# Reordering first loads and sums, merging a normalization, and doing sums on two tiles at a time, in a transformer block bound by the matrix engine

## The chip, the cores and the metric

One core of a Trainium2 chip runs the whole kernel. The metric is the device time of one execution in microseconds (us). PE is TensorE (matmuls; PEld its weight loads), DVE is VectorE, ACT is ScalarE, POOL is GpSimd, SP is the engine that issues most DMAs. Every execution in this document but one was in the fast state (granted TensorE clock 0.999 or 1.0); the exception is named where it comes.

## The reference, cut to what matters

```python
def reference(A_x, A_wqkv, A_wo, B_x, B_w_gate, B_w_up, B_w_down):
    # x is 2048 x 1024 bf16; 32 heads; a window of 8 keys with dilation 2; feed-forward width 3584
    h  = x + attention(layernorm(x))  @ wo
    h2 = h + ((layernorm(h) @ w_gate) * (layernorm(h) @ w_up)) @ w_down
    return h2
```

The kernel works in four chunks of 512 rows. It does part of the feed-forward products with Strassen-like sums: 7 products of half-size blocks in place of 8, at the price of sums of weight blocks and of activation blocks. Those sums are the subject here.

## The kernel before: the parts concerned

The start loads four row tiles on SP's queue and the first weight block in two halves on ACT's queue, then normalizes, transposes (on PE) and copies one row tile after the other.

```python
    for t in range(4):
        load_x0(t)
    load_w0(0, 4)                                   # ACT's queue
    nc.scalar.preload_act_table_set("natural_log_exp_and_others")
    load_w0(4, 4)                                   # ACT's queue
    # ... 13 warm-up matmuls ...
    def first_rstd(t):
        nc.vector.bn_aggr(out=mv0[:, t, :], in_=sts[t][:])
        rstd_of(mv0, rs0, t, t + 1)                 # Ln and Exp on ACT

    def first_norm(t):
        lns[t] = lnp.tile([128, D], BF, tag="ln", name=f"ln0_{t}")
        for i in range(2):
            cols = bass.ts(i, 512)
            nc.vector.tensor_scalar(lns[t][:, cols], x0[t][:, cols], mv0[:, t, 0:1], rs0[:, t:t + 1],
                                    ALU.subtract, ALU.mult)

    def first_transpose(t):
        for hf in range(2):
            # ... 4 transposes of 128 x 128 on PE into pt ...
            nc.scalar.copy(lnTs[0][:, bass.ts(hf, 4), bass.ts(t, 128)], pt[:])
```

The head of the pair stage. `weight_sums` scales a weight block on ACT and makes four sums of its quarters on DVE; `activation_sums` makes four sums of the quarters of the transposed, normalized rows, which come from DMA transposes. `result` reads a PSUM tile, adds, and stores the output.

```python
    for q in range(2):
        dprod(ex[q], q, EF["21"], fcells(dn["12"]), False)
        # ...
    retire(1)
    activation_sums(l2, l3, dn["px"])
    weight_sums(0, nc.vector)
    for q in range(2):
        dprod(ey[q], q, EF["12"], fcells(dn["22"]), False)
        nc.vector.tensor_tensor(p5t[:, q, :], p5t[:, q, :], hs1[q][:, 512:1024], ALU.add)
        result(1, hs1[q], q, 1, ey[q], dn["inv"], p5t[:, q, :])
    for q in range(2):
        dprod(ex[q], q, EF["22"], fcells([dn["kx"], dn["vx"]]), False)
        result(1, hs1[2 + q], 2 + q, 0, ex[q], dn["inv"], None)
```

The last stage. `HA` holds 14 tiles of 128 x 512 in each of four quadrants; `HF` are the same bytes as f16.

```python
    for k in range(NP):                             # NP = 14
        to_f16(HF["22"][k], HA["22"][k], sh)        # DVE
        to_f16(HF["21"][k], HA["21"][k], sh)
    # ... conversion of "11" on ACT; S1 = HF21 + HF22 on DVE, 14 sums ...
    for q in range(4):
        dprod(ps_x[q], q, HA["12"], fcells(down["b21"]), False)
        result(2, hs2[q], q, 0, ps_x[q], scale_d.inv, None)
    for k in range(NP):
        nc.vector.tensor_tensor(HF["21"][k], HF["11"][k], HF["21"][k], ALU.subtract)
    for k in range(NP):
        nc.vector.tensor_tensor(HF["11"][k], S1[k], HF["11"][k], ALU.subtract)
    sub(t2h, down["b22"], t1h)                      # prodx, two halves
    # ... four products with S1 ...
    for q in range(4):
        dprod(ps_y[q], q, HF["11"], fcells(t2h), False)        # "dy"
```

## Time and profile before

| | before |
|---|---|
| time, median of 5 runs | 779.04 us (778.85 to 779.19) |
| span of the profiled run | 777.6 us |
| PE busy | 770.7 us, 99% |
| DVE / ACT busy | 614.9 us, 79% / 473.8 us, 61% |

The page cuts the span into 40 slices; each digit is a tenth of busy time, and the second line is the granted clock.

```profile
PE   8999999999999999999999999999999999999998
...
PEclk9999999999999999999999999999999999999999
```

PE is never visibly idle but in the first and the last slice. What can be won without taking matmuls away is therefore small, and it must be looked for in single waits. A matmul of 512 columns is drawn 0.379 us long though the next one starts 0.216 us after it, so a busy PE hides short waits. Where this document says that PE **lost** time at a place, it is worked out from start times: start of the matmul, less start of the one before, less 0.216 us (0.056 us for 128 columns). Beyond 18 us, the trace before has losses of over 0.03 us in five places only: 0.14 at 60.6 us, 1.04 and 0.39 ahead of the two `pv` products at 520 us, 0.24 and 0.43 in the first `dy` product at 725 us.

The chain that ended last (start, us, what):

```profile
694.99 18.14 PE dx L787 x84
...
718.60 2.01 DVE hq L1066 x6
...
727.22 10.73 PE dy L787 x49
```

The chain runs on PE up to 713.1, leaves it for DVE, and comes back to PE at 727.22. That detour is the place where the kernel waits for sums.

### The profile page before, as it was taken

Reading aid. Unit: us, or ns where it says so; the run is one execution under the profiler, and the core shown is the slowest. Engines: PE = TensorE matmul, PEld = TensorE weight load, DVE = VectorE, ACT = ScalarE, POOL = GpSimd, SP = SyncE. Lnnn points to the kernel's source line nnn. Section 1 sums busy time; section 2 is a strip of 40 time slices with the busy share of each in tenths; the row PEclk is TensorE's granted clock in tenths of the full one; section 3 lists DMA queues with packets and bytes.
Section 4 is the critical chain, followed back from the end, with each engine's and each line's share of the span. In section 5 each row is a group of like instructions: output and inputs, shape, how many; then the busy total and the mean of one; then the engine's idle time right before and its main releaser. Section 6 shows DMA issues by size and latency. Waiting matters only on the chain.

```text
span 777.6 us, 10495 instructions
## 1 busy us (share of the span) xinstructions
PE 770.7 (99%) x3707; PEld 355.1 (46%) x3707; DVE 614.9 (79%) x805; ACT 473.8 (61%) x1029; POOL 142.3 (18%) x152
## 2 busy tenths in 40 slices
PE   8999999999999999999999999999999999999998
PEld 6544444444444444444444444444444444444444
DVE  6619999999899999999988989985553444579862
ACT  4627445323476661976769899746677677788240
POOL 0000000010000200002000001008778687600000
PEclk9999999999999999999999999999999999999999
DMA  8999693895965868867645384744332423730001
GB/s 275 258 217 222 158 291 88 255 305 130 338 205 167 269 228 239 267 225 259 207 150 192 120 298 121 162 96 111 106 97 67 109 62 101 248 131 28 1 27 55
DMA packets 181605, 133.86 MB, mean 172 GB/s; under 512 B 79024, under 2 KB 174384, under 8 KB 179504
## 3 DMA queue, kind: packets, MB, share of 16 engines
q1 hardware_dynamic: 176912, 110.12, 50.1%
q0 software_dynamic: 3584, 22.02, 8.1%
q10 hardware_dynamic: 1056, 1.05, 0.4%
q8 instruction: 29, 0.48, 0.3%
q14 instruction: 24, 0.20, 0.1%
HBM read 104.86 MB, written 22.02 MB: 163 GB/s over the span
## 4 chain that ended last, share of the span: by engine, by line
PE 88%; DVE 9%; DMA 1%; ACT 1%; issue 0%; SPq 0%; ACTq 0%; DVEq 0%
PE ps L392 20%; PE pg L392 12%; PE pu L392 12%; PE dx L787 6%; PE pz L680 6%; PE acc L626 6%; PE py L680 6%; PE px L680 6%; PE wo L513 4%; PE pv L680 3%; PE dy L787 3%; DVE h L834 1%; DMA w_qkv<-in_A_wqkv_dram 1%; PE ps L353 1%; PE ex L787 1%; DVE prodx L780 1%
## 5 line engine op out<-in xcount | busy, mean ns | idle before, releaser
L392 PE MATMUL ps<-lnT,w_qkv 128*128 128x512 bf16 x736 | 159.8, 379 | 0.0
L392 PEld LDWEIGHTS <-w_qkv 128*128 128x128 bf16 x736 | 71.8, 98 | 86.0 <-issue 0.3
L392 PE MATMUL pg<-lnT,w_wg 128*128 128x512 bf16 x448 | 105.8, 379 | 0.0
L392 PE MATMUL pu<-lnT,w_wu 128*128 128x512 bf16 x448 | 105.8, 379 | 0.0
L304 ACT CAST sg<-ps 128x512 bf16<-128x512 f32 x96 | 54.8, 590 | 52.7 <-PE ps L392 50.0
L475 DVE TENSOR_TENSOR pv<-vD,at 128x4096 bf16<-128x4096 bf16 x32 | 72.5, 2287 | 0.3
L432 DVE TENSOR_TENSOR prod<-qD,kD 128x4096 bf16<-128x4096 bf16 x32 | 72.3, 2284 | 0.1
L680 PEld LDWEIGHTS <-sw 128*128 128x128 f16 x448 | 43.8, 98 | 54.3 <-issue 1.7
L392 PEld LDWEIGHTS <-w_wg 128*128 128x128 bf16 x448 | 43.8, 98 | 52.9
L392 PEld LDWEIGHTS <-w_wu 128*128 128x128 bf16 x448 | 43.8, 98 | 52.9
L596 ACT CAST us<-pu 128x512 bf16<-128x512 f32 x56 | 33.2, 593 | 40.5 <-PE pu L392 40.4
L680 PE MATMUL px<-lnT,ws 128*128 128x512 bf16 x224 | 55.2, 379 | 0.0
L680 PEld LDWEIGHTS <-ws 128*128 128x128 f16 x336 | 32.9, 98 | 39.6
L626 PE MATMUL acc<-w_wd,gs 128*128 128x512 bf16 x224 | 48.5, 379 | 0.0
L487 POOL DMA_DIRECT2D od<-oD x4 | 2.2, 544 | 252.8 <-DVE oD L485 162.5
L661 POOL TENSOR_TENSOR sw<-ws 128x512 f16<-128x512 f16 x26 | 30.0, 1153 | 85.4 <-PE py L680 78.2
L185 ACT ACTIVATE rs<-mv,eps 128x1 f32<-128x1 f32 (+1 forms) x25 | 7.4, 297 | 52.6 <-DVE mv L182 49.2
L591 ACT CAST gs<-pg 128x512 bf16<-128x512 f32 x56 | 32.9, 587 | 10.7 <-PE pg L392 8.7
L434 DVE TENSOR_TENSOR prod<-prod 128x4096 bf16<-128x4096 bf16 x16 | 36.6, 2288 | 0.3
L541 ACT ACTIVATE junkd<-w_wd 128x512 bf16<-128x512 bf16 x56 | 34.3, 618 | 0.0
L626 PEld LDWEIGHTS <-gs 128*128 128x128 bf16 x224 | 21.9, 98 | 26.4
L697 ACT COPY py<-px 128x512 f32<-128x512 f32 x28 | 16.0, 570 | 26.2 <-PE px L680 26.2
(312 smaller groups left out, 1400.5 us busy)
## 6 DMA issues: line engine op xcount, KB each, us to landing
w_wg<-in_B_w_gate_dram SPq DMA_DIRECT2D x14, 1024.0 KB, 6.7
w_wu<-in_B_w_up_dram SPq DMA_DIRECT2D x14, 1024.0 KB, 5.4
w_wd<-in_B_w_down_dram SPq DMA_DIRECT2D x8, 896.0 KB, 8.8
w_pair<-in_B_w_gate_dram SPq DMA_DIRECT2D x14, 512.0 KB, 4.1
w_pair<-in_B_w_up_dram SPq DMA_DIRECT2D x14, 512.0 KB, 5.4
w_wo<-in_A_wo_dram SPq DMA_DIRECT2D x6, 1024.0 KB, 8.1
w_qkv<-in_A_wqkv_dram SPq DMA_DIRECT2D x5, 1024.0 KB, 9.1
kd<-sg SPq DMA_DIRECT2D x32, 144.0 KB, 3.0
```

What stands on the lines that cost most here:

```text
L304: nc.scalar.copy(sg[:, HB:HB + TC], ps[:])
L392: nc.tensor.matmul(ps[:], lhsT=wt[:, ko, bass.ts(j, 128)], rhs=rhs[:, ko, :], start=(ko == 0), stop=(ko == KO - 1))
L432: nc.vector.tensor_tensor(prod[:, j], qD[:], kD[:, :, o:o + SUB], ALU.mult)
L434: nc.vector.tensor_tensor(prod[:, :, 0:16], prod[:, :, 0:16], prod[:, :, 16:32], ALU.add)
L475: nc.vector.tensor_tensor(pv[:, j], vD[:, :, o:o + SUB], at[:, w, None, :].to_broadcast((128, DH, SUB)), ALU.mult)
L513: nc.tensor.matmul(ps[:], lhsT=oTs[c][:, kk, t, :], rhs=wts["wo", c, hf][:, kk, :], start=(kk == 0), stop=(kk == KO - 1))
L541: nc.scalar.activation(junk, src, ACTF.Abs, accum_out=self.l1[:, k:k + 1])
L591: nc.scalar.copy(gs[:], pg[:])
L596: nc.scalar.copy(us[:], pu[:])
L626: nc.tensor.matmul(acc[t][:], lhsT=hT[f][:, bass.ts(t, 128)], rhs=wts["wd", c, hf, b][:, j, :], start=(f == 0), stop=(f == NF - 1))
L680: nc.tensor.matmul(ps[:], lhsT=lhs[:, ko, :], rhs=rhs[:, ko, :], start=(fresh and ko == 0), stop=(ko == 3), skip_group_check=not fresh)
L787: nc.tensor.matmul(ps[:, bass.ds(lo, n)], lhsT=lhs[k][:, bass.ts(q, 128)], rhs=rhs[k][:, bass.ds(lo, n)], start=(fresh and k == 0), stop=( ...
```

## The change

Its intent: issue both weight halves before ACT is given the table load; normalize row tiles 1 to 3 in one instruction instead of two; let the first weight sums, whose inputs are ready sooner, go ahead of the activation sums on DVE; and handle those of the last stage's tiles that lie in pairs (3 pairs in each quadrant, 8 single tiles) two at a time, to save instructions.

```diff
     load_w0(0, 4)
+    load_w0(4, 4)
     nc.scalar.preload_act_table_set("natural_log_exp_and_others")
-    load_w0(4, 4)
@@ first_norm
-        for i in range(2):
-            cols = bass.ts(i, 512)
+        for cols in (bass.ts(0, 512), bass.ts(1, 512)) if t == 0 else (slice(0, D),):
@@ head of the pair stage
+    weight_sums(0, nc.vector)
     activation_sums(l2, l3, dn["px"])
-    weight_sums(0, nc.vector)
@@ last stage
+    GA = {k: HA[k][0:8] + [ht[:, r::4, :] for ht in rooms] for r, k in enumerate(("11", "21", "12", "22"))}
+    GF = {k: [f16(a) for a in GA[k]] for k in GA}
+    NG = len(GA["11"])
...  (conversions and the sums into S1 likewise; G1 is S1 with its last six tiles as three pairs)
-    for k in range(NP):
-        nc.vector.tensor_tensor(HF["21"][k], HF["11"][k], HF["21"][k], ALU.subtract)
-    for k in range(NP):
-        nc.vector.tensor_tensor(HF["11"][k], S1[k], HF["11"][k], ALU.subtract)
+    for k in range(NG):
+        nc.vector.tensor_tensor(GF["21"][k], GF["11"][k], GF["21"][k], ALU.subtract)
+    for k in range(NG):
+        nc.vector.tensor_tensor(GF["11"][k], G1[k], GF["11"][k], ALU.subtract)
```

## The prediction

> **What bounds the kernel now.** I read the page first, then the list of PE's waits, then the chain that ended last, then the timeline of the three places where PE waits. The engine line and the list of waits say almost all of it:
>
> ```profile
> PE 770.7 (99%) x3707; PEld 355.1 (46%) x3707; DVE 614.9 (79%) x805; ACT 473.8 (61%) x1029; POOL 142.3 (18%) x152
> ...
> PE warm_ps L298 <- DVE warm L284: 1.2, 1, 1.2
> PE pv L680 <- DVE h L792: 1.1, 2, 0.9
> PE ps L353 <- ACT lnT L348: 0.3, 1, 0.3
> PE pt L347 <- DVE ln L340: 0.3, 1, 0.3
> PE ps L353 <- DMA w_qkv<-in_A_wqkv_dram: 0.3, 1, 0.3
> PE dy L787 <- DVE prodx L780: 0.3, 1, 0.3
> ```
>
> The columns of the waits are total us, how many, longest. TensorE is the bound everywhere: granted clock 1.00, matmuls 0.216 us apart (8 take 1.73 us in the chain), and only some 3.5 us of waiting shown in 777.6. A page's busy PE hides short waits, because a 512-wide matmul is drawn 0.379 us long while the next starts 0.216 us after it; so I work with start times below. The diff has no matmul added or removed, and the comparison of the instruction streams shows PE's order unchanged. The change can therefore win only what PE waits in three places: the start, the head of the pair stage (pv), and the last stage (dy).
>
> The pair stage's head, from the timeline of that stretch (start, length, what, idle before and its releaser):
>
> ```profile
> 507.38 3.69 ACT L654 ACTIVATE ws<-w_pair,sbgu 128x4096 f16<-128x4096 bf16 x1
> ...
> 511.90 1.23 DVE L672 TENSOR_TENSOR prodx<-lnT,lnT 128x2048 f16<-128x2048 bf16 x1 [2.19 <-DMA out_dram<-h]
> ...
> 516.57 0.69 DVE L661 TENSOR_TENSOR sw<-ws 128x1024 f16<-128x1024 f16 x1
> ...
> 519.89 0.75 DVE L792 SCALAR_TENSOR_TENSOR h<-ey,inv_h1d,ep 128x512 bf16<-128x512 f32 x1
> ...
> 520.69 1.02 PE L680 MATMUL pv<-prodx,sw 128*128 128x512 f16 x4 [0.88 <-DVE h L792]
> ...
> 522.81 1.02 PE L680 MATMUL pv<-prodx,sw 128*128 128x512 f16 x4 [0.23 <-DVE h L792]
> ```
>
> The scaled weights ws are ready at 511.07 (507.38 + 3.69), but DVE stands idle from 509.7 to 511.90, because next in its order are the activation sums, whose inputs (the transposed rows of chunk 3, last issued at about 509.8) have not landed. The releaser is printed as an output store; transposes of the same queue take 3.1 to 3.6 us to landing, so I take it for them. Then DVE runs without a gap: four sums, four weight sums, an add, and the result h at 519.89, which empties the PSUM bank that pv needs. PE could have begun pv at 519.65 (517.92 + 8 x 0.216) and begins at 520.69.
>
> The start and the end, same columns; the last two lines are from the chain (start, us, what):
>
> ```profile
> 11.44 0.73 DVE L340 TENSOR_SCALAR ln<-x,mv,rs 128x512 bf16<-128x512 bf16 x2 [0.37 <-ACT rs L186]
> 11.91 0.72 PE L347 MATMUL pt<-ident,ln 128*128 128x128 bf16 x8
> 12.35 1.07 ACT L348 COPY lnT<-pt 128x512 bf16<-128x512 bf16 x2 [0.94 <-PE pt L347]
> 13.31 0.31 ACT L185 ACTIVATE rs<-mv,eps 128x1 f32<-128x1 f32 x1
> ...
> 722.62 0.67 DVE kx L1066 x2
> 723.30 3.88 DVE prodx L780 x2
> ```
>
> At the start each row tile goes round a loop: normalize, transpose, copy, then the next tile's Ln and Exp on ScalarE, then normalize. It turns in 2.44 us (copies at 9.91, 12.35, 14.79). At the end DVE, busy from 713.16, finishes prodx at 727.17, and dy's eighth matmul starts at 727.22.
>
> **What the Trainium skill says.** (1) "VectorE: DVE Perf Modes", in the section on the TRN2 errata, gives SBUF operations a fixed cost per instruction, about 58 + elements/accel cycles at 0.96 GHz. For a two-source 16-bit add (accel 2) that is 0.327 us for 512 and 0.594 for 1024. The trace agrees: adds of 512 follow each other every 0.335 us (two in 0.67, above), adds of 1024 every 0.605 (weight sums). (2) "Perfetto Trace Analysis", section Optimizing Scalar/DVE Operations, says that larger operations help a saturated engine, but that where an engine only causes bubbles on others, breaking instructions up may finish work sooner. The second half applies to the start, and the change does the opposite there. (3) "ScalarE: Activation LUTs", section What ACT_TABLE_LOAD costs, has about 1283 ns for the load and 1380 ns of drain. The trace has 1.28 us for the load (at 1.24), but the second weight DMA was issued at 1.27, beside it, not after it. (4) "DMA: Bandwidth & Descriptors", section Issuing engines are not separate DMA queues, says that all issues end on the same 16 engines; the trace shows 370 to 410 GB/s while x and the first weights load.
>
> **The change part by part.**
>
> *Weight block ahead of the table load.* The first half's issue takes 0.75 to 1.21, so the second can go at about 1.21 instead of 1.27: 0.06 us. It landed at 8.98, 7.7 us after its issue, with the 2 MB of x and weights that share the engines; the bandwidth sets that, not the issue. The table load moves to about 1.7 and ends at 3.0, while the first Ln runs at 5.60. **Worth 0.0.**
>
> *Normalizing in one instruction for tiles 1 to 3.* The two halves end 0.73 us after their start, the first after 0.405; one instruction of 1024 takes 0.539 (median of the same operation at line 190). The second half is 0.19 earlier, the first 0.135 later, and PE's transposes and the copies begin with the first. Tile 1: normalize starts at 8.93, so the transposes could go at 9.40 and go at 9.48, when PE has finished the matmuls that the weight DMA held; now 8.93 + 0.54 + 0.065 = 9.535, +0.055. Tile 2: 11.44 + 0.055 + 0.605 = 12.10 for 11.91, +0.19. Tile 3: 13.88 + 0.19 + 0.605 = 14.68 for 14.35, +0.33. The shorter second half wins nothing, since the second copy waits for ScalarE (0.48 us behind the first) and not for its transposes. All later matmuls move along. **Costs 0.33.**
>
> *Weight sums ahead of the activation sums.* DVE starts when ws is ready, 511.12, not at 511.90. Four weight sums take 2.54 (516.57 to 519.11), so the activation sums run from 513.66, when their inputs have long landed, and take 4.67 (511.90 to 516.57). The add starts at 518.33 for 519.11: 0.78 earlier, and so do h and the following results. pv starts at 519.91 (its slot is 519.65), the second pv at 522.03 for 522.81 (its slot would be 521.64). PE's loss here falls from 1.43 (1.04 + 0.39) to 0.65. **Worth 0.78**, and PE runs without a wait from there to the last stage, so it is kept.
>
> *Sums on two tiles at a time.* 6 of the 14 tiles of each quadrant become 3 pairs. Conversions on DVE: two of 512 cost 0.54 (hq: 12 in 3.23), one of 1024 about 0.40, so 6 pairs save 0.8; the first sums save 0.2; ScalarE's conversions 0.2 (1.24 to 1.17 a pair). All this lies before 713.16, where DVE waits 1.08 us for PE's last product whatever it saved, so it is worth nothing. Behind it lie two loops on the path, lines 1064 and 1066: 3 pairs each, 0.67 becoming 0.605: 6 x 0.065 = 0.39. prodx ends at 724.84 and 726.78. dy's first matmul then starts in its slot, 725.04 (was 725.28), and its eighth at 726.83 for 727.22; the slot would be 726.55. **Worth 0.39.** The fourth loop (line 1087, 750.75 to 755.4) is wanted only at 761.96 and is hidden.
>
> Sum: +0.33 - 0.78 - 0.39 = -0.84. From 779.04: **778.2 us**.
>
> **The rivals.** (a) *The start wins instead.* If the weight half came distinctly sooner, PE would do its 8 held matmuls sooner. But tile 1 then waits for the one-piece normalize at 9.535, so it can bring nothing; only if a 1024 normalize gave its result sooner than 0.54 us would the start be even: total 777.9. (b) *The activation sums become the wait at pv.* They end at 518.33 instead of 516.57, but the slot of pv is 519.65, so 1.3 us remain; a slip of the weight conversion on ScalarE would eat the gain directly: 779.0 if all is lost. (c) *Strided pairs lose the fast mode.* The pair tiles have two rows of 512 spaced 2048 apart. Line 661 already reads strided pieces of 128 at 0.605 for 1024, which speaks against it. If it happened, 6 adds would take about 1.1 instead of 0.605 and the end would lose about 2.6: 781.2. (d) *Everything moves within noise*: 779.0. Nothing here makes 2% (15.6 us); all PE waits together are about 3.5.
>
> **Range and chances.** The three terms have errors of about 0.2 each, and the runs before spread over 0.34. With the start even, 777.9 or a little less; with half of the pair's gain lost, 778.6. I take 777.6 to 778.8. Within 2%: 0.985.
>
> **What would show each step.** Right: DVE's first weight sum at about 511.4 (511.1 plus the start's 0.33), pv's wait under 0.3, dy's wait smaller, the copies of the first row tiles at 9.97, 12.54 and 15.12, the first 512-wide matmul at 17.54 instead of 17.21. Wrong: copies still 2.44 apart (then the merged normalize costs nothing); the weight half landing well before 8.9; a weight sum still starting after 511.9; adds of 2 x 512 at over 0.7; or a new PE wait in the last stage.

## The result, and the profile after

| | before | after |
|---|---|---|
| median of 5 runs | 779.04 us | 778.30 us |
| lowest to highest | 778.85 to 779.19 | 778.02 to 778.39 |
| span of the profiled run | 777.6 us | 776.5 us |

The changed kernel is 0.74 us faster by the medians. A ratio here is the mean time of one kernel's fast runs over that of the other's in the same rounds, so not quite the ratio of the medians: 0.999, with a 95% interval of 0.9975 to 1.0005. By that interval alone it is "the same"; the two sets of five runs do not overlap, though, and the traces say where the 0.74 lies.

PE's waits in the changed kernel (total us, how many, longest), to be held against the six lines in the prediction:

```profile
PE warm_ps L298 <- DVE warm L284: 1.2, 1, 1.2
PE ps L352 <- ACT lnT L347: 0.5, 1, 0.5
PE pv L679 <- DVE h L791: 0.2, 1, 0.2
```

The wait at `pv` went from 1.1 us in two pieces to 0.2 in one, and the one at `dy` is no longer listed (0.25 us is still lost there, hidden under the drawn length of the matmul before). The timeline of the pair stage's head:

```profile
507.48 3.69 ACT L653 ACTIVATE ws<-w_pair,sbgu 128x4096 f16<-128x4096 bf16 x1
...
511.20 0.69 DVE L660 TENSOR_TENSOR sw<-ws 128x1024 f16<-128x1024 f16 x1 [1.39 <-ACT ws L653]
...
513.74 1.22 DVE L671 TENSOR_TENSOR prodx<-lnT,lnT 128x2048 f16<-128x2048 bf16 x1
...
519.20 0.75 DVE L791 SCALAR_TENSOR_TENSOR h<-ey,inv_h1d,ep 128x512 bf16<-128x512 f32 x1
...
520.00 1.02 PE L679 MATMUL pv<-prodx,sw 128*128 128x512 f16 x4
```

DVE now starts as soon as ACT has the scaled weights (507.48 + 3.69 = 511.17), and the first activation sum at 513.74 no longer waits for its transposes. The result `h` comes at 519.20 instead of 519.89, `pv` at 520.00 instead of 520.69. PE's slot for it was 519.78 (first `px` at 518.05 plus 8 x 0.216), so 0.23 us is still lost, and 0.39 at the second `pv`.

The start, same columns as before:

```profile
11.44 0.55 DVE L339 TENSOR_SCALAR ln<-x,mv,rs 128x1024 bf16<-128x1024 bf16 x1 [0.62 <-ACT rs L186]
...
12.05 0.62 PE L346 MATMUL pt<-ident,ln 128*128 128x128 bf16 x8
...
12.48 1.07 ACT L347 COPY lnT<-pt 128x512 bf16<-128x512 bf16 x2 [1.07 <-PE pt L346]
...
14.62 0.62 PE L346 MATMUL pt<-ident,ln 128*128 128x128 bf16 x8
```

The normalization starts at 11.44 in both traces, but the transposes come 0.61 us later instead of 0.47, and the loop turns in 2.57 us (12.05 to 14.62) instead of 2.44 (11.91 to 14.35).

The chain at the end:

```profile
715.88 0.60 DVE hq_o L1069
716.48 0.60 DVE lx L1069
717.09 0.60 DVE kx L1069
...
722.18 3.88 DVE prodx L779 x2
...
726.10 10.73 PE dy L786 x49
```

Each pair takes 0.60 us of the chain where two tiles took 0.67, so a 2 x 512 pair with its strided rows runs at the rate of a plain 1024.

Setting matmul n of one trace against matmul n of the other (both have 3707, in the same order) gives the whole difference by place: +0.26 us up to the first 512-wide matmul (17.21 to 17.47), -0.14 at 60.6, -0.81 at `pv`, -0.42 at `dy`, in sum -1.11, the difference of the two spans. The -0.14 is at a place that the change does not edit (what varies there is told at the end of the point-by-point part); the trace before is one of the slower runs of its kernel (779.41 us). The experiments tell what of this is the change.

### The profile page after: what moved, and what is told of

It reads as the page before. It is cut to its first block, busy times and chain, and to the rows that moved or that the text cites. A ratio compares the mean times of both kernels' runs of the same rounds, so it can differ in the third digit from the quotient of the medians.

```text
span 776.5 us, 10462 instructions
## 1 busy us (share of the span) xinstructions
PE 771.1 (99%) x3707; PEld 355.5 (46%) x3707; DVE 612.6 (79%) x784; ACT 472.6 (61%) x1023; POOL 142.1 (18%) x152
## 4 chain that ended last, share of the span: by engine, by line
PE 90%; DVE 9%; ACT 1%; issue 0%; DVEq 0%
PE ps L391 20%; PE pu L391 12%; PE pg L391 12%; PE dx L786 6%; PE pz L679 6%; PE acc L625 6%; PE py L679 6%; PE px L679 6%; PE wo L512 4%; PE pv L679 3%; PE dy L786 3%; DVE h L833 1%; PE ps L352 1%; PE ex L786 1%; DVE prodx L779 1%; DVE w_dn L779 1%
```

## The experiments

Four kernels each carry one part of the change alone. Each was timed in five rounds beside the kernel before on the same chip. All differences are far below 2%, and only the intervals of after_halves, best and best_mid lie wholly below 1. For the single parts the gain or cost is therefore read from the places in the traces; the medians only agree with it.

**w_only.** The weight block's second half ahead of the table load, nothing else.

```diff
     load_w0(0, 4)
+    load_w0(4, 4)
     nc.scalar.preload_act_table_set("natural_log_exp_and_others")
-    load_w0(4, 4)
```

> Before, with the weight block's second half issued ahead of the table load and nothing else. Theory (each part acts in its own place, the wait for the weight half is set by the shared DMA bandwidth): the second half lands at 8.85 to 8.98 us instead of 8.98, PE's wait before its second group of first matmuls shrinks by at most 0.1, tile 1's transposes start at 9.40 to 9.48, and the time is 0.0 to 0.1 us shorter. Rival (the table load held the issue up, so the half comes much sooner): it lands before 8.5 and the time falls by 0.3 or more.

Measured: 779.19 us against 779.14 (ratio 1.0003, interval 0.999 to 1.0016): no change. PE, which waits for the half at this place, went on at 8.75 us, and in the other traces in which it stands there it went on at 8.42, 8.46, 8.47, 8.92, 8.97 and 9.03 with the old order and at 8.47, 8.53 and 8.92 with the new. The list of waits names the weight DMA in four of these traces only, so some of the times are upper bounds for the landing. The landings themselves, which the traces also hold, were at 8.71 here, 8.37 to 8.98 in the seven traces with the old order, and 8.10 to 8.88 in the other five with the new. The two orders share one spread of half a microsecond, and no gain of the new order is to be seen in it; a gain of 0.1, the most that was expected, is below what these runs resolve. This trace also lost 0.57 us at 60.7, where the trace before lost 0.14: scatter in a place that was not edited.

**norm_only.** The normalization of tiles 1 to 3 in one instruction, nothing else.

```diff
-        for i in range(2):
-            cols = bass.ts(i, 512)
+        for cols in (bass.ts(0, 512), bass.ts(1, 512)) if t == 0 else (slice(0, D),):
```

> Before, with the normalization of tiles 1 to 3 in one instruction and nothing else. Theory: it costs 0.25 to 0.35 us, because the transposes wait for the whole row: they start about 0.6 us after the normalization's start instead of 0.47, for tiles 2 and 3 (12.05 and 14.62 instead of 11.91 and 14.35), and the first 512-wide matmul starts at about 17.47 to 17.54 instead of 17.21. Rival (a shorter total lets the next tile start sooner): the loop stays at 2.44 us or less and the time is the same or up to 0.2 shorter.

Measured: 779.49 us against 779.14, 0.35 longer by the medians (ratio 1.0005, interval 0.9992 to 1.0019), though the two sets of runs overlap. Its timeline:

```profile
11.47 0.55 DVE L339 TENSOR_SCALAR ln<-x,mv,rs 128x1024 bf16<-128x1024 bf16 x1 [0.62 <-ACT rs L186]
...
12.07 0.45 PEld L346 LDWEIGHTS <-ln 128*128 128x128 bf16 x8 [0.17 <-DVE ln L339]
...
14.64 0.45 PEld L346 LDWEIGHTS <-ln 128*128 128x128 bf16 x8 [0.17 <-DVE ln L339]
```

The last column names the new wait: PE stands 0.17 us for the whole row, twice. From the first matmul of tile 1 to the first 512-wide matmul there are 6.92 or 6.93 us in the three traces with the merged normalization (this one, the changed kernel's two) and 6.66 in the nine that have it in halves and are otherwise alike there. **At the start this part of the change costs 0.26 to 0.27 us, against its intent**, and that is the steadiest figure.

**sums_only** and **sums_only_2.** The weight sums ahead of the activation sums, nothing else.

```diff
+    weight_sums(0, nc.vector)
     activation_sums(l2, l3, dn["px"])
-    weight_sums(0, nc.vector)
```

> Before, with the pair's first weight sums ahead of its activation sums and nothing else. Theory: 0.78 to 0.83 us shorter; PE's lost time ahead of the two pv products falls from 1.04 + 0.39 to about 0.25 + 0.39, and no other wait appears. Rival (the activation sums, now last, become the wait, or the gain is given back later in the pair stage): under 0.4 us shorter, with a PE wait on an activation sum or a weight sum of the next block.

The first run's profiled execution took 1015.66 us at a granted clock of 0.753. That execution counts in no ratio and says nothing of the waits. The median of 778.47 us counts it; the four fast executions alone have a median of 778.35 against 779.14. The same kernel was run once more.

> The first run's profile fell at a granted clock of 0.753, so it says nothing of the waits: the same kernel (before, with only the weight sums ahead of the activation sums) once more for a trace in the fast state. Theory: 0.6 to 0.85 us shorter; PE's lost times at pv 0.2 to 0.3 and 0.39, against 0.7 to 1.04 and 0.39 in the traces with the old order; no wait that the other traces don't have; the dy waits of 0.24 and 0.43 unchanged. Rival: a new wait in the pair stage takes over half of the gain back.

Measured: 778.35 against 778.96 us, 0.61 shorter; the four fast executions of the first run were 0.79 shorter. The new trace's waits:

```profile
PE dy L787 <- DVE prodx L780: 0.3, 1, 0.3
PE pv L680 <- DVE h L792: 0.2, 1, 0.2
```

PE lost 0.23 and 0.39 us at `pv`, exactly as in the changed kernel, and the `dy` waits are untouched (0.24 and 0.43). No other wait took over, so the rival falls. What varies is the old order: in its seven traces the first `pv` lost 1.04, 1.01, 0.92, 0.90, 0.90, 0.81 and 0.71 us, because there DVE waits for the DMA transposes and they land at slightly different times (DVE idle 1.86 to 2.19 us ahead of the first activation sum, which starts 0.28 us after the last transpose has landed in every one of the seven). The mean is 0.90, so the reordering is worth 0.90 - 0.23 = 0.67 us on average and up to 0.81 against the slowest trace. It also takes the scatter away: with the new order the loss is 0.23 or 0.24 in all four traces.

**pairs_only.** All sums and conversions of the last stage on two tiles at a time, nothing else (the diff above, last part).

> Before, with all sums and conversions of the last stage on two tiles at a time and nothing else. Theory: 0.39 to 0.43 us shorter, all of it at the head of the dy products (PE's lost time there 0.67 before, about 0.25 now). Rival (less work on VectorE, 2.3 us of busy time in all, is what counts): 0.8 us or more shorter, with the product before it starting or ending sooner too.

Measured: 778.64 us against 779.14, 0.50 shorter by the medians, though the two sets of runs overlap. PE lost nothing at the first matmul of `dy` and 0.25 at the eighth, against 0.24 and 0.43. To see which sums carry this, the pairing was split in two:

**pairs_on_path**: only the two subtraction loops behind the stage's last result are paired; conversions, sums into S1 and the last loop stay single.

```diff
-    for k in range(NP):
-        nc.vector.tensor_tensor(HF["21"][k], HF["11"][k], HF["21"][k], ALU.subtract)
-    for k in range(NP):
-        nc.vector.tensor_tensor(HF["11"][k], S1[k], HF["11"][k], ALU.subtract)
+    for k in range(NG):
+        nc.vector.tensor_tensor(GF["21"][k], GF["11"][k], GF["21"][k], ALU.subtract)
+    for k in range(NG):
+        nc.vector.tensor_tensor(GF["11"][k], G1[k], GF["11"][k], ALU.subtract)
```

> Before, with only the two subtraction loops behind the last product of the stage (those that make the left side of dy) on two tiles at a time. Theory: these two loops are all that counts of the pairing: 0.39 to 0.43 us shorter, as with all of it. Rival (the conversions and the first sums carry the gain): no change.

**pairs_off_path**: the other way round, these two loops single and all the rest paired.

> Before, with only the conversions, the first sums and the last subtraction loop on two tiles at a time, the two loops on the path left single. Theory: VectorE has about 1.7 us less to do, its idle time ahead of the stage's last result grows by about 1 us, and the time stays within 0.1 of before; PE still loses 0.67 at dy. Rival: 0.3 or more shorter.

Measured in the same rounds: pairs_on_path 778.22, pairs_off_path 778.88, before 778.88 us. The first keeps the gain at `dy` (0.25 lost), the second has none of it (0.24 and 0.43 lost) and no change of the time. The 0.66 of the first is more than the 0.42 that its trace shows at `dy`; the rest is the scatter of some 0.2 between sets of runs. DVE's timeline in pairs_off_path shows where the saved work went:

```profile
708.48 2.07 DVE L792 SCALAR_TENSOR_TENSOR h<-dx,ibd,h 128x512 bf16<-128x512 f32 x3
712.61 0.75 DVE L792 SCALAR_TENSOR_TENSOR h<-dx,ibd,h 128x512 bf16<-128x512 f32 x1 [2.06 <-PE dx L787]
```

and before:

```profile
710.02 2.06 DVE L792 SCALAR_TENSOR_TENSOR h<-dx,ibd,h 128x512 bf16<-128x512 f32 x3
713.16 0.75 DVE L792 SCALAR_TENSOR_TENSOR h<-dx,ibd,h 128x512 bf16<-128x512 f32 x1 [1.08 <-PE dx L787]
```

This trace is 0.55 us ahead of the other at this place. Beyond that, DVE is done about a microsecond sooner and waits that much longer (2.06 instead of 1.08 us) for PE's last product. Saved work ahead of a wait turns into wait.

**after_halves.** The changed kernel with the normalization in halves again, that is, without the part that costs.

```diff
-        for cols in (bass.ts(0, 512), bass.ts(1, 512)) if t == 0 else (slice(0, D),):
+        for i in range(2):
+            cols = bass.ts(i, 512)
```

> The changed kernel with the normalization of tiles 1 to 3 in halves again. Theory: 0.25 to 0.35 us shorter than the changed kernel, so 1.0 to 1.1 shorter than before; the first 512-wide matmul starts at 17.1 to 17.25. Rival (merged and split cost the same, the 0.26 shift seen in the changed kernel's trace came from its warm-up matmuls): no difference to the changed kernel.

Measured: 777.73 us against 778.88 before: 1.15 shorter (ratio 0.9986, interval 0.9974 to 0.9999), 0.4 more than the changed kernel gains. Its first 512-wide matmul was at 16.69, sooner than expected, but so it was in before_again; the whole start moves with the landing of the first row tile (DVE's first statistics began anywhere between 3.52 and 4.03 us in 13 traces). The duration within the start, 6.66 us, is what tells.

**before_again.** The kernel before, unchanged, as a control.

> The kernel before, unchanged, as a control of what one trace differs from another. Theory: PE's lost times at pv (1.04 and 0.39) and at dy (0.24 and 0.43) come back within 0.03, while the 0.14 lost at 60.6 and the landing of the weight half (8.98) move by 0.1 or so. Rival (the places differ from run to run as much as the change moved them): pv or dy differ by 0.2 or more.

Measured: 778.70 us against 778.88 in the same rounds, which is how far two medians of one kernel differ here. PE lost 1.01 and 0.38 at `pv`, 0.25 and 0.43 at `dy`, and nothing at 60.6. The control agrees within 0.03, but that was luck for the first `pv`, as the six other traces with the old order show.

**after_again.** The changed kernel once more.

> The changed kernel once more, on the same chip and in the same rounds as the two versions to compare with it. Theory: 0.7 to 0.8 us under before; PE's lost times at pv 0.23 and 0.39, at dy 0.25, tile 2's and 3's transposes 0.16 each, as in its first trace.

Measured: 778.22 us against 779.01: 0.79 shorter, with PE losing 0.23 and 0.39 at `pv` and 0.25 at `dy`, as in its first trace, and 0.31 at 60.6, which its first trace did not have.

**best.** The traces leave three waits after the start: 0.23 and 0.39 at `pv`, both for results that empty a PSUM bank, and 0.25 at `dy`, for a chain of DVE work that begins only after the last result of the stage, ahead of which DVE is idle. This version keeps the change, puts the halves back, and moves DVE's work accordingly:

```diff
@@ activation_sums: t1 and t2 at once, t3 and t4 in a function that is called later
     for q in range(2):
         dprod(ex[q], q, EF["22"], fcells([dn["kx"], dn["vx"]]), False)
         result(1, hs1[2 + q], 2 + q, 0, ex[q], dn["inv"], None)
+    late_sums()                                     # t3, t4
@@ last stage
     for q in range(4):
         dprod(ps_x[q], q, HA["12"], fcells(down["b21"]), False)
+        if q == 3:
+            for k in range(NG):
+                nc.vector.tensor_tensor(GF["21"][k], GF["11"][k], GF["21"][k], ALU.subtract)
         result(2, hs2[q], q, 0, ps_x[q], scale_d.inv, None)
-    for k in range(NG):
-        nc.vector.tensor_tensor(GF["21"][k], GF["11"][k], GF["21"][k], ALU.subtract)
```

> The changed kernel with halves in the normalization again, with the results that empty the PSUM banks put ahead of the last two activation sums, and with the first subtraction loop of the last stage put ahead of that stage's last result. Theory: PE's two waits at pv (0.23 and 0.39) and the one at dy (0.25) go, and 0.26 at the start: 1.1 us shorter than the changed kernel, 1.9 to 2.0 shorter than before, about 777.1. Rival (other operations take the freed places as the wait: the third activation sum at pz, the result's bank at the dx products): under 0.6 shorter than the changed kernel, with a new PE wait at pz or dx.

Measured: 776.93 us against 779.01 before and 778.22 for the changed kernel in the same rounds: 2.08 and 1.29 shorter (ratio to before 0.9974, interval 0.9962 to 0.9987). What was to go adds up to 1.13 against the changed kernel (0.23, 0.39, 0.25 and 0.26 at the start); the rest of the 1.29 is within the scatter between sets of runs. The parts of this edit were not timed apart; that each wait is gone is read from the trace. All of PE's waits in this kernel:

```profile
PE warm_ps L298 <- DVE warm L284: 1.2, 1, 1.2
PE ps L353 <- ACT lnT L348: 0.5, 1, 0.5
```

and the head of the pair stage:

```profile
516.60 0.75 DVE L795 SCALAR_TENSOR_TENSOR h<-ey,inv_h1d,ep 128x512 bf16<-128x512 f32 x1
...
519.43 1.03 PE L683 MATMUL pv<-prodx,sw 128*128 128x512 f16 x4
...
520.03 1.22 DVE L677 TENSOR_TENSOR prodx<-lnT 128x2048 f16<-128x2048 bf16 x1
```

The bank is emptied at 517.35, two microseconds before `pv` wants it, and `pv` starts in its slot (517.70 + 8 x 0.216 = 519.43). The later sums still come in time. After the first 18 us PE loses nothing over 0.03 us anywhere in this trace. The chain around the last place is PE alone:

```profile
705.00 18.56 PE dx L790 x86
723.56 6.48 PE dy L790 x30
```

**best_mid.** The same, with the next tile's Ln and Exp on ACT between the two copies of a tile, to shorten the loop of the start.

```diff
             nc.scalar.copy(lnTs[0][:, bass.ts(hf, 4), bass.ts(t, 128)], pt[:])
+            if hf == 0 and t < 3:
+                first_rstd(t + 1)
```

> The kernel best with the next tile's Ln and Exp between the two copies of a tile at the start. Theory: normalization of tiles 2 and 3 starts about 0.45 us sooner, PE is then the bound there and the loop turns in about 2.25 to 2.30 us instead of 2.44: 0.2 to 0.3 us shorter than best. Rival (the second copy, now 0.5 us later, becomes PE's wait, or the statistics are not ready): the same or longer than best.

Measured: 777.16 us against 776.93 for best: no gain, the expectation missed. The normalization did start 0.5 us sooner after the first copy (9.77 to 10.82, against 9.91 to 11.44 before), but the loop turns in 2.40 us, not 2.25 to 2.30:

```profile
12.18 0.58 ACT L348 COPY lnT<-pt 128x512 bf16<-128x512 bf16 x1 [0.92 <-PE pt L347]
...
14.58 1.07 ACT L348 COPY lnT<-pt 128x512 bf16<-128x512 bf16 x2 [0.92 <-PE pt L347]
```

PE now has 40 matmuls of 0.056 us per tile (2.24 us) without a wait for DVE, but 0.17 us ahead of each tile's first product, for the first copy. The wait moved from the normalization to the copy. The loop won 0.07 us in all (6.59 from tile 1's first matmul to the first 512-wide one, against 6.66), and best stays the version to keep.

## Why the prediction was right, point by point

- **The sum.** Expected -0.84 us; measured -0.74 and -0.79 in two sets of runs. The prediction's 778.2 met 778.30. That it came so near is in part luck: place by place the traces give +0.26, -0.67 and -0.42 where +0.33, -0.78 and -0.39 were predicted, so that the errors of -0.07, +0.11 and -0.03 cancel, and sets of runs differ by some 0.2 among themselves.
- **The signs.** The first weight sum began at 511.20 (about 511.4 predicted), the copies at 9.91, 12.48 and 15.05 (9.97, 12.54 and 15.12), the first 512-wide matmul at 17.47 (17.54). Of the signs of being wrong, only a weight half well before 8.9 was seen (8.48 in the changed kernel's second trace), and the old order has that too (8.42 in before_again).
- **Weight block.** Predicted 0.0: right. w_only shows 0.05 the other way, within the scatter. The table load started at 1.80 and ended at 3.08, long before the first Ln at 5.53. That the half lands when the shared engines are through was argued; shown is only that the order does not move PE's start beyond its spread of 8.4 to 9.0. (Over the load the trace has 359 to 410 GB/s; the prediction read 370 to 410.)
- **Normalization.** Predicted +0.33; norm_only +0.35 by its medians, its trace +0.27. The mechanism, transposes 0.61 after the start instead of 0.47, was as predicted, 0.13 for each of tiles 2 and 3. The 0.055 for tile 1 did not show beside the 0.5 us by which the start moves from run to run. Rival (a), that the start wins, falls.
- **Weight sums.** Predicted 0.78, on the one trace that there was. Mechanism and remaining wait were right (0.65 left predicted, 0.62 measured), but the term has the largest error of the four: 0.67 on average over the traces, 0.61 and 0.79 by the medians of fast runs. The step that was off is taking the transposes' landing of that one trace, the latest of seven against `pv`'s slot, for the usual one. Rival (b) falls: the last activation sum ended at 518.49, 1.29 us before `pv`'s slot. That the printed releaser, an output store, stands for the transposes is borne out by the trace before: the last transpose, issued from 508.49 on and not at 509.8, landed at 511.62, DVE's wait for its semaphore ended at 511.66, and the wait for the semaphore that the store uses had ended at 509.01, before the store was issued.
- **Pairs.** Predicted 0.39, all behind the stage's last result; measured 0.42 in the trace, 0.50 by the medians of pairs_only. The eighth `dy` matmul lost 0.25, 0.28 predicted. That the rest of the pairing is worth nothing is shown by pairs_off_path. Rival (c), strided pairs at a slower rate, falls: 0.60 us a pair.
- **Rival (d)**, noise, falls by the two sets of five runs that do not overlap, and by the places.
- **The place at 60.6 us.** The traces tell why some of them lose 0.14 to 0.57 us there and others nothing. A cast on ACT empties the PSUM bank that PE wants (w_only's list of waits names it); ahead of it in ACT's order stand the Ln and Exp of three row tiles of the next chunk, which wait for DVE's statistics. In all 13 traces the cast ends 5.37 or 5.38 us after the first of these row tiles has landed (53.8 to 55.5 us), and PE goes on 0.05 us after the cast, or in its slot if that is later. This gives the loss of every trace within 0.02 us. The tile landed at 55.15 in the trace before and at 55.16 in the changed kernel's first, so the -0.14 is the other side of the merged normalization: the start that came 0.26 later moved PE's slot to 0.10 us after the point at which the cast let it go. A later start costs nothing where PE would have waited anyway.

## What to carry to other kernels

With the bound engine 99% busy, each part of this change was worth what it took from that engine's few waits, so list those waits and ask of each part whether it lies behind one. Merging instructions paid where a chain of them ended last (0.42 us), was lost ahead of a wait for the bound engine, and cost where a consumer could have started on the first half (0.26 us). On an engine that works in order, put first what is ready first, and put the operation that frees another engine's buffer ahead of those that are wanted later.

## What the Trainium skill lacked or had wrong

- "VectorE: DVE Perf Modes", section on the TRN2 errata: estimates from its 58 + elements/accel cycles meet the spacing of adds well (0.327 and 0.594 us; the runs show 0.335 and 0.605), but neither of the page's two fixed terms gives how long one such operation lasts. For the normalization of 1024, at 4 elements a cycle, the 58 cycles give an estimate of (58 + 256)/0.96 = 0.327 us, and the fixed term of about 150 cycles that the page names for a single operation one of 0.42; the instruction lasted 0.55, and PE started 0.61 after its beginning.
- The same section sets its mitigation at tiles of 512 elements or more. Sums of 512 meet that, and doing them on 1024 still won 0.42 us in a chain; and the section does not say what is lost where a consumer waits for the first half (0.26 us here). "Perfetto Trace Analysis", section Optimizing Scalar/DVE Operations, has the second case, without a number.
- "ScalarE: Activation LUTs", section What ACT_TABLE_LOAD costs: the section does not say that a DMA issue behind a table load in ACT's order need not wait for it. Here the load ran from 1.24 to 2.52 us and the issue behind it went at 1.27.
- No page that I used has how far DMA landings scatter from run to run: the first row tile's statistics began between 3.52 and 4.03 us, and the wait for the transposed rows was 1.86 to 2.19 us, in executions of kernels that differ little or not at all up to there. A term read from one trace carries that error.
